# Reordering the first batch's heads, hashes and bursts in a hash-attention and max-out FFN kernel, with four smaller edits

## The chip, the cores and the metric

One NeuronCore of a Trainium2 chip runs the whole program, in one launch. The metric is the device time of one execution, in microseconds. The kernel before takes 272.56 us in the median of three runs (272.11 to 272.76).

## What is computed

Attention over 4 batches, 8 heads, 768 rows and 64 dimensions, in which a query sees only the keys that fall in its own hash bucket, and then a feed-forward network (FFN) that takes the maximum of three products.

```python
q_bits = (np.einsum('bhsd,dk->bhsk', q, proj) > 0)      # 6 bits; the same for k
mask = q_bucket[:, :, :, None] == k_bucket[:, :, None, :]
scores = np.where(mask, scale * q @ k.T, -1e9)
attn = softmax(scores) @ v
x = attn.transpose(0, 2, 1, 3).reshape(B * S, H * D)    # 3072 x 512
out = maximum(maximum(x @ w1, x @ w2), x @ w3) @ w_out   # 512 -> 768 -> 512
```

## The kernel before

**Units.** The work on the scores is cut into 192 units, 48 a batch. A unit is one head, one chunk of queries and a part of the keys. In batch 0 a chunk has 256 queries (three chunks, two units for each head and chunk), in the later batches 384 (two chunks, three units). `scores(u)` (L279) multiplies keys by queries on TensorE into one of two PSUM buffers `sc` (L295), and ScalarE takes the exponential into one of 24 tiles `AT` (L303). The hash bits, as +0.5 and -0.5, stand as 6 or 8 more rows under the 64 dimensions in the S tiles, so that one product gives score and mask together. Each AT tile also has, behind each block of columns, columns of ones, with which a burst sums V. Their place depends on the width of the chunk: a tile that first served 256 wide blocks gets new ones by a memset when it first serves 384 wide ones (L300 to L302, on VectorE, just ahead of the exponential).

**Order of the units** (L258, L259): in batch 0 heads 0 to 3 one after the other, each with its three chunks, then heads 4 to 7 chunk by chunk; later batches go chunk by chunk.

**Getting heads ready.** In batch 0 queries and keys come in pairs of heads 0 to 3: TensorE turns them (`pair_turn`, L122), VectorE or ScalarE copies them (`pair_keep`, L131, L129), GpSimd narrows them into the S tiles (`pair_place`, L136), and a hash makes the bits: `head_rest` for one head (L169 on TensorE, four L174 on VectorE) or `pair_hash` for a pair (L149, L152, then four DMAs by SyncE, L158). Later heads come in quads of four: loads by GpSimd or SyncE (L194), 32 x 32 transposes on VectorE (`turn`, L200), narrowing on GpSimd (L205), placing by DMA on SyncE (L210), and `quad_hash` (L219, L222, four DMAs at L230).

**Bursts.** When four heads of a chunk have their exponentials, a burst makes the row sums (`sums`, L350, then L357 to L361 on VectorE) and the products with V in two sides (`values`, L372, then L379). The second side gives back the AT tiles. In batch 0 the bursts of heads 0 to 3 go in three pieces each, at hand-set units. From batch 1 on VectorE first adds the three parts of a head (`add`, L326, from chunk 5 on also L329), so that `sums` has less to do.

**FFN.** `ffn_groups(c)` (L390) makes 18 groups of four matmuls (L401) for a chunk, each with a copy or maximum after it (L406, L408, L410), then halves of three matmuls with the output weights (L445). A group takes one of four PSUM banks `ms`, as do turns, hashes and bursts.

**The order written out by hand** stands from L460 on. A prologue brings head 0; then for each unit u the loop issues `scores(u + 1)`, what `when(u, ...)` has put down for u, about one FFN group (credit 1, later 1.15 a unit), and the burst pieces due at u. A quad's hash is issued at the end of its unit, its DMAs in the next. Every engine works through its own instructions in that order. After the loop come the last burst, the FFN groups left over, and the FFN of the last chunk. `SPREAD` sets at which units the quads of batches 2 and 3 are transposed.

Of the kernel before, what the change touches and what calls it, by code (L numbers as in the profile page):

```python
# [17 lines left out]
def kernel(  # L18
# [12 lines left out]
    nc = tc.nc  # L31
    B, H, S, D = q.shape
# [3 lines left out]
    HALF = S // 2  # L36
# [14 lines left out]
    SCALE = 0.125 / (RS * RS)  # L51
    EPS = 2.0 ** -60
    NAT = 24
    SPREAD = {2: (61, 9), 3: (100, 12)}
    THIRD_ADD = 5
    LAG = (1, 4)
    ATW = 776
# [36 lines left out]
    def give(i):  # L94
        free_banks.append(i)
# [159 lines left out]
    def parts_of(c):  # L255
        return chunks[c][2] * NM // (2 * HALF)

    order = [(c, h) for h in range(4) for c in range(3)] + [(c, h) for c in range(3) for h in range(4, H)]  # L258
    order += [(c, h) for c in range(3, NCH) for h in range(H)]  # L259
    units = [(c, h, n) for c, h in order for n in range(parts_of(c))]  # L260
    NU = len(units)
# [76 lines left out]
    def burst(c, i):  # L338
# [24 lines left out]
        def values(side, m0, m1):  # L363
# [10 lines left out]
            if m1 == NM:  # L374
                if first:
                    sv_of[b, i, side] = small.tile([P, 1], FP32, tag=f"sv{side}", name="sv")
                    nc.vector.tensor_scalar(out=sv_of[b, i, side][:], in0=av[:, w : w + 1], scalar1=EPS, scalar2=None,
                                            op0=AluOp.mult)
                nc.vector.scalar_tensor_tensor(out=xt_of(c)[:, 2 * i + side, 0:w], in0=av[:, 0:w],  # L379
                                               scalar=sv_of[b, i, side][:], in1=rb[0][:, 0:w], op0=AluOp.add, op1=AluOp.mult)  # L380
                give(held[side][0])
                if side == 1:
                    for h in range(4 * i, 4 * i + 4):
                        for n in range(parts_of(c)):
                            at_free.append(at_of[unit_at[c, h, n]])

        return sums, values

# [71 lines left out]
    with tc.manual_schedule():  # L460
# [41 lines left out]
        head_hash(mk, 0, 1, 0, (1,))  # L502
        head_bits(mk, 0, 1, 0, 1)
        give(ik)
        scores(0)
        pair_turn(0, 1, 1, bk)
        head_hash(mq, 0, 0, 0, (1,))
        head_bits(mq, 0, 0, 0, 1)
        give(iq)
        pair_turn(0, 0, 1, bq)  # L510
        pair_keep(0, 1, 1, bk)
        give(ib)
# [6 lines left out]
        for x in range(4):  # L519
            nc.gpsimd.tensor_copy(pj[x * Q : (x + 1) * Q, :, x : x + 4 * NBITS - 3 : 4], pst[:])  # L520

        for pi, us in ((1, ((0, 1, 0), (0, 0, 0), (3, 1, 1), (4, 0, 1))), (2, ((6, 1, 0), (7, 1, 1), (8, 0, 0), (9, 0, 1))),
                       (3, ((13, 1, 0), (14, 1, 1), (15, 0, 0), (16, 0, 1)))):
            for u, side, hd in us:
                when(u, pair_group, pi, side, hd, nc.scalar if pi == 1 and hd == 1 else None)
                if pi == 1:
                    for par in range(2):
                        when(u, pair_place, pi, side, par, hd, hd + 1)
                elif hd == 1:
                    for par in range(2):  # L530
                        when(u, pair_place, pi, side, par)
        when(2, head_rest, 0, 1)
        when(2, t32.pop, 0)
        when(5, head_rest, 1, 0)
        when(10, pair_hash, 2)
        when(11, t32.pop, 2)
        when(11, head_rest, 1, 1)
        when(12, t32.pop, 1)
        when(17, pair_hash, 3)
        when(18, t32.pop, 3)  # L540
        when(17, load_v, 1)
        for n, u in ((0, 3), (1, 12), (2, 21), (3, 31)):
            when(u, load_weights, n)
# [4 lines left out]
        for g in range(2, NQUAD):  # L548
            b2, i2 = divmod(g, 2)
            need = UPB * b2 + 12 * i2  # L550
            for n, side in enumerate((1, 0)):
# [9 lines left out]
                    if n2 % 2:  # L561
                        when(u2 + 1, narrow, name, n2 // 2)
                when(us[3] + 3, place, name, range(4))
            hash_at[{2: 33, 3: 47}.get(g, need - 9)] = g
            when({2: 36, 3: 46}.get(g, need - 22), load_v, g)

        ffn, credit = [], 0
# [2 lines left out]
        for c, i in sorted(done_at, key=lambda e: done_at[e]):  # L570
# [1 line left out]
            sums, values = burst(c, i)  # L572
            pieces = [lambda f=sums: f(0, NM), lambda f=values: f(0, 0, NM), lambda f=values: f(1, 0, NM)]
            for n, f in enumerate(pieces):
                u = {(0, 0): (20, 21, 22), (1, 0): (24, 25, 26), (2, 0): (28, 29, 30)}.get((c, i), (d, d, d))[n]
                todo.setdefault(u, []).append(f)
            last_of[c] = max(u, last_of.get(c, 0))
        ffn_at = {}
# [5 lines left out]
                when(min(u + 2, NU - 1), add, c, h, n)  # L584

        for u in range(NU):
            if u + 1 < NU:
                scores(u + 1)
            for f in at.pop(u, []):
                f()  # L590
# [10 lines left out]
            if u in hash_at:  # L601
                when(u + 1, quad_hash(hash_at[u]))

        for u in sorted(todo):
            for f in todo[u]:
                f()
# [33 lines left out]
```

## Time and profile before

| what | value |
| --- | --- |
| median of 3 runs | 272.56 us |
| the profiled execution's own time | 272.63 us |
| its span, first to last instruction | 270.9 us |
| TensorE matmuls busy | 259.4 us |
| VectorE busy | 208.9 us |
| ScalarE busy | 177.6 us |
| GpSimd busy | 68.4 us |
| granted TensorE clock | 1.000 |

In the profile, PE is TensorE's matmuls, PEld its weight loads, DVE VectorE, ACT ScalarE, POOL GpSimd and SP SyncE. L295 is line 295 of the kernel before. A row of the timeline gives the start, the time from start to end, engine and line, the operation, output and inputs by the program's names, and how many instructions of the same kind are merged; in brackets stands how long the engine was idle before it, and what ended that. The ends of matmuls are modelled and overlap the next start, so that a price of TensorE work is taken from one start to the next. A row of waits gives who waited for whom, the total in us, how often, and the longest. A row of windows gives the stretch, its length, and then the busy time of PE, PEld, DVE, ACT and POOL, the granted clock, the busy share of the DMA engines and GB/s. A row of DMA issues ends with the median time from issue to landing.

### The profile page before, as it was taken

To read this page: it belongs to the slowest core of one execution; us is meant where nothing else is said; L and a number is where in the kernel's file an instruction comes from. 1 tells how busy PE (TensorE), PEld (TensorE's weight loads), DVE (VectorE), ACT (ScalarE), POOL (GpSimd) and SP (SyncE) were. 2 spreads that over 40 slices of the span, in tenths; PEclk is the share of its full clock that TensorE was granted. 3 is DMA by queue.
4 is the path that set the end of the run, shared out by engine and by line. 5 is a ranking of instruction groups with operands and counts; after the bars stand their busy time and mean duration, and the time that the engine had idled before them with its cause. 6 is when DMAs were issued, how large, how long until landed. Compare 5 with 4: busy or idle time off the path is not lost.

```text
span 270.9 us, 6455 instructions
## 1 busy us (share of the span) xinstructions
PE 259.4 (96%) x2505; PEld 154.5 (57%) x2505; DVE 208.9 (77%) x517; ACT 177.6 (66%) x257; POOL 68.4 (25%) x108
## 2 busy tenths in 40 slices
PE   7899999999989999979999999999999999998995
PEld 3555567865756575545555555565555655554553
DVE  2777686967699899948999998799849795887351
ACT  3587776676939693963959768484895859580322
POOL 3489641272032435140141512011000000000000
PEclk9999999999999999999999999999999999999999
DMA  6969999959623863980036291801130003000303
GB/s 204 315 137 160 221 255 229 229 80 250 150 72 88 156 173 38 235 218 20 11 91 202 30 205 69 169 11 46 29 116 2 2 2 116 2 0 2 116 0 116
DMA packets 20717, 30.95 MB, mean 114 GB/s; under 512 B 2608, under 2 KB 15248, under 8 KB 20688
## 3 DMA queue, kind: packets, MB, share of 16 engines
q0 software_dynamic: 8128, 13.37, 26.3%
q1 hardware_dynamic: 12128, 16.66, 21.1%
q10 hardware_dynamic: 432, 0.52, 0.5%
q8 instruction: 19, 0.31, 0.5%
q14 instruction: 10, 0.08, 0.1%
HBM read 25.17 MB, written 6.29 MB: 116 GB/s over the span
## 4 chain that ended last, share of the span: by engine, by line
PE 86%; DVE 5%; ACT 3%; DMA 2%; POOL 2%; issue 1%; SPq 0%; DVEq 0%; ACTq 0%; POOLq 0%
PE ms L401 32%; PE sc L295 22%; PE ms L372 11%; PE ms L445 10%; PE ms L350 3%; PE ms L219 3%; ACT AT L303 3%; DMA S<-bits 2%; PE ms L483 1%; POOL S L136 1%; PE ms L149 1%; PE ms L122 1%; DVE ad L326 1%; PE ms L169 1%; DVE S L174 1%
## 5 line engine op out<-in xcount | busy, mean ns | idle before, releaser
L303 ACT ACTIVATE AT<-sc 128x768 f16<-128x768 f32 x192 | 152.7, 816 | 65.6 <-PE sc L295 57.9
L401 PE MATMUL ms<-xT,w_sb 128*128 128x384 f16 (+1 forms) x648 | 115.0, 307 | 0.0
L295 PE MATMUL sc<-S 72*128 72x384 bf16 (+1 forms) x432 | 93.5, 308 | 5.4 <-ACT AT L303 2.5
L401 PEld LDWEIGHTS <-w_sb 128*128 128x128 f16 x648 | 62.6, 97 | 35.8 <-issue 0.3
L410 DVE TENSOR_TENSOR ht<-ht,ms 128x384 f16<-128x384 f16 (+1 forms) x108 | 54.2, 504 | 26.0 <-PE ms L401 23.1
L295 PEld LDWEIGHTS <-S 72*128 72x128 bf16 (+1 forms) x432 | 39.4, 98 | 38.0 <-issue 14.1
L205 POOL TENSOR_SCALAR T<-T 128x768 bf16<-128x768 f32 x24 | 22.9, 953 | 105.2 <-DVE T L200 64.5
L372 PE MATMUL ms<-AT,vo 128*32 128x385 f16 (+3 forms) x864 | 35.5, 309 | 0.0
L445 PE MATMUL ms<-wout_sb,ht 128*128 128x512 f16 x138 | 35.3, 378 | 0.0
L372 PEld LDWEIGHTS <-vo 128*32 128x32 f16 x864 | 22.8, 96 | 10.5 <-issue 2.9
L326 DVE TENSOR_TENSOR ad<-ad,AT 128x768 f16<-128x768 f16 x48 | 26.6, 553 | 1.8 <-ACT AT L303 1.1
L200 DVE STREAM_TRANSPOSE T<-nat 128x384 f32<-128x384 f32 x48 | 26.9, 565 | 0.0
L326 DVE TENSOR_TENSOR ad<-AT,AT 128x768 f16<-128x768 f16 x48 | 26.2, 546 | 0.4 <-ACT AT L303 0.4
L406 ACT CAST ht<-ms 128x384 f16<-128x384 f32 x36 | 17.2, 477 | 8.8 <-PE ms L401 8.8
L379 DVE SCALAR_TENSOR_TENSOR xT<-ms,sv,rb 128x384 f16<-128x384 f32 (+1 forms) x36 | 19.8, 567 | 1.6 <-PE ms L372 0.2
L445 PEld LDWEIGHTS <-ht 128*128 128x128 f16 x138 | 13.3, 97 | 13.0 <-DVE ht L410 0.4
L449 ACT COPY osb<-ms 128x512 f32<-128x512 f32 x21 | 12.2, 582 | 8.3 <-PE ms L445 7.2
L329 DVE TENSOR_TENSOR ad<-ad 128x384 f16<-128x384 f16 x32 | 15.5, 484 | 1.1
L136 POOL TENSOR_SCALAR S<-T 64x384 bf16<-64x384 f32 (+1 forms) x23 | 14.2, 617 | 4.7 <-DVE T L131 3.1
L357 DVE STREAM_TRANSPOSE ys<-ms 128x384 f32<-128x384 f32 (+1 forms) x18 | 9.6, 535 | 6.5 <-PE ms L350 6.4
L174 DVE TENSOR_SCALAR S<-ms 6x384 bf16<-6x384 f32 x16 | 8.9, 554 | 3.8 <-PE ms L169 3.5
L194 POOL DMA_DIRECT2D nat<-in_q_dram x20 | 11.1, 564 | 2.1 <-DMA vo<-in_v_dram 2.0
(48 smaller groups left out, 122.8 us busy)
## 6 DMA issues: line engine op xcount, KB each, us to landing
out_dram<-osb SPq DMA_DIRECT2D x21, 256.0 KB
S<-T SPq DMA_DIRECT2D x48, 96.0 KB
nat<-in_q_dram POOLq DMA_DIRECT2D x20, 192.0 KB, 7.3
vo<-in_v_dram POOLq DMA_DIRECT2D x8, 384.0 KB, 6.4
nat<-in_k_dram POOLq DMA_DIRECT2D x16, 192.0 KB, 6.5
w_sb<-in_moe_w_dram POOLq DMA_DIRECT2D x3, 768.0 KB, 7.6
nat<-in_k_dram SPq DMA_DIRECT2D x10, 192.0 KB
nat<-in_k_dram SPq DMA_DIRECT2D x3, 384.0 KB
```

The costliest lines, as they stand in the source:

```text
L136: nc.gpsimd.tensor_scalar(out=o, in0=i_, scalar1=RS, scalar2=1.0, op0=AluOp.mult, op1=AluOp.mult)
L200: nc.vector.transpose(t32[name][:, u, half * HALF : (half + 1) * HALF], i_)
L205: nc.gpsimd.tensor_scalar(out=t16[name][:, u, :], in0=t32[name][:, u, :], scalar1=RS, scalar2=1.0, op0=AluOp.mult, op1=AluOp.mult)
L295: nc.tensor.matmul(views[j], s_of[kn][0 : D + bits, kx, m * P : (m + 1) * P], s_of[qn][0 : D + bits, qx, q0 : q0 + w], start=True, stop=True)
L303: nc.scalar.activation(t[:, :, 0:w], whole, ActFn.Exp, bias=-SCALE * 0.25 * bits, scale=SCALE)
L326: nc.vector.tensor_tensor(out=sum_of[c, h][:], in0=t[0], in1=t[n], op=AluOp.add)
L372: nc.tensor.matmul(av[Q * x : Q * (x + 1), 0:n], v_at[2 * b + i][:, x, cb * D + side : (cb + 1) * D : 2], weights_of(c, 4 * i + x, m)[:, 0 ...
L379: nc.vector.scalar_tensor_tensor(out=xt_of(c)[:, 2 * i + side, 0:w], in0=av[:, 0:w], scalar=sv_of[b, i, side][:], in1=rb[0][:, 0:w], op0=A ...
L401: nc.tensor.matmul(ps[:, 0:w], w_sb[wi][:, jc, fb * P : (fb + 1) * P], xt[:, jc, 0:w], start=(jc == 0), stop=(jc == NJC - 1))
L406: nc.scalar.copy(hts[fb][:, 0:w], ps[:, 0:w])
L410: nc.vector.tensor_tensor(out=hts[fb][:, 0:w], in0=hts[fb][:, 0:w], in1=ps[:, 0:w], op=AluOp.max)
L445: nc.tensor.matmul(ps[:, 0:DM], hts[fb][:, tb * P : (tb + 1) * P], wout_sb[:, fb, :], start=(fb == 0), stop=(fb == NFB - 1))
```

## The change

In batch 0, heads 2 and 3 go chunk by chunk, so that the first chunk's four heads are done at unit 15 in place of 19, and the second's at 19 in place of 21. The first three bursts, in nine pieces, move from units 20 to 30 to units 16 to 29. The turns of pair 2's queries move one unit back and those of pair 3 one or two units forward; the hash of head 3 (`head_rest`, pair 1, second head) moves from unit 11 to 8, that of pair 2 from 10 to 12, that of pair 3 from 17 to 18. In the prologue the second half of head 0's query hash goes ahead of the first scores, and the scores of unit 1 go ahead of head 1's turns.

Four edits stand outside this: the transposes of batch 3 start three units earlier; the columns of ones of the 384 wide blocks are written by GpSimd, right after the burst that gives the tile back, for 24 tiles; the hashes of quads 4 to 7 go 12 units ahead of their first use in place of 9; and after the loop three FFN groups go ahead of the last burst.

```diff
-    SPREAD = {2: (61, 9), 3: (100, 12)}
+    SPREAD = {2: (61, 9), 3: (97, 12)}
...
-    order = [(c, h) for h in range(4) for c in range(3)] + [(c, h) for c in range(3) for h in range(4, H)]
+    order = [(c, h) for h in range(2) for c in range(3)] + [(c, h) for c in range(3) for h in (2, 3)]
+    order += [(c, h) for c in range(3) for h in range(4, H)]
...
                 if side == 1:
                     for h in range(4 * i, 4 * i + 4):
                         for n in range(parts_of(c)):
-                            at_free.append(at_of[unit_at[c, h, n]])
+                            a = at_of[unit_at[c, h, n]]
+                            if b == 0 and i == 1:
+                                nc.gpsimd.memset(blocks(at_tiles[a], HALF)[:, :, HALF : HALF + 2], 1.0)
+                                at_form[a] = HALF
+                            at_free.append(a)
...
         head_bits(mk, 0, 1, 0, 1)
         give(ik)
-        scores(0)
-        pair_turn(0, 1, 1, bk)
         head_hash(mq, 0, 0, 0, (1,))
         head_bits(mq, 0, 0, 0, 1)
         give(iq)
+        scores(0)
+        scores(1)
+        pair_turn(0, 1, 1, bk)
         pair_turn(0, 0, 1, bq)
...
-        for pi, us in ((1, ((0, 1, 0), (0, 0, 0), (3, 1, 1), (4, 0, 1))), (2, ((6, 1, 0), (7, 1, 1), (8, 0, 0), (9, 0, 1))),
-                       (3, ((13, 1, 0), (14, 1, 1), (15, 0, 0), (16, 0, 1)))):
+        for pi, us in ((1, ((0, 1, 0), (0, 0, 0), (3, 1, 1), (4, 0, 1))), (2, ((6, 1, 0), (7, 1, 1), (9, 0, 0), (10, 0, 1))),
+                       (3, ((11, 1, 0), (13, 1, 1), (14, 0, 0), (15, 0, 1)))):
...
-        when(10, pair_hash, 2)
-        when(11, t32.pop, 2)
-        when(11, head_rest, 1, 1)
-        when(12, t32.pop, 1)
-        when(17, pair_hash, 3)
-        when(18, t32.pop, 3)
+        when(8, head_rest, 1, 1)
+        when(9, t32.pop, 1)
+        when(12, pair_hash, 2)
+        when(13, t32.pop, 2)
+        when(18, pair_hash, 3)
+        when(19, t32.pop, 3)
...
-            hash_at[{2: 33, 3: 47}.get(g, need - 9)] = g
+            hash_at[{2: 33, 3: 47}.get(g, need - 12)] = g
...
-                u = {(0, 0): (20, 21, 22), (1, 0): (24, 25, 26), (2, 0): (28, 29, 30)}.get((c, i), (d, d, d))[n]
+                u = {(0, 0): (16, 17, 20), (1, 0): (21, 22, 24), (2, 0): (26, 27, 29)}.get((c, i), (d, d, d))[n]
...
-            if u + 1 < NU:
+            if 0 < u < NU - 1:
                 scores(u + 1)
...
+        for f in ffn[:3]:
+            f()
+        ffn = ffn[3:]
         for u in sorted(todo):
             for f in todo[u]:
                 f()
```

## The prediction

> **What bounds the kernel now.** I read the page first, for the engine that carries the span, then the waits of TensorE, then the places where it stood still.
>
> ```profile
> PE 259.4 (96%) x2505; PEld 154.5 (57%) x2505; DVE 208.9 (77%) x517; ACT 177.6 (66%) x257; POOL 68.4 (25%) x108
> ```
> ```profile
> PE sc L295 <- ACT AT L303: 2.5, 4, 1.2
> PE sc L295 <- DMA S<-bits: 1.7, 1, 1.7
> ```
> TensorE bounds the span at 259.4 of 270.9 us, and the change leaves its matmuls as they are. So it can win only idle time: the waits in its timeline, of which the view of waits puts these two first, and idle time that the modelled ends of matmuls hide. The 2.5 us on ScalarE stand at four places; these two the change touches:
>
> ```profile
> 64.22 0.49 PE L295 MATMUL sc<-S 72*128 72x384 bf16 x2 [0.43 <-ACT AT L303]
> ```
> ```profile
> 81.50 0.48 PE L295 MATMUL sc<-S 72*128 72x384 bf16 x2 [1.22 <-ACT AT L303]
> ```
> The hidden part lies in the first batch. Busy time by stretch, 12.4 to 42.6 us (span, then PE, PEld, DVE, ACT, POOL) and, for later, 73.3 to 113.7:
>
> ```profile
> 12.40:42.60 30.20, 29.32 (x445) 18.59 (x442) 23.15 (x55) 23.77 (x33) 22.21 (x37) 1.00 0.98 199
> 73.30:113.70 40.40, 38.83 (x397) 25.02 (x395) 37.92 (x101) 27.60 (x37) 15.33 (x21) 1.00 0.55 121
> ```
> The first row calls TensorE busy for 29.32 of 30.20 us. Priced from one start to the next, its work is less:
>
> ```profile
> 11.62 0.83 PE L169 MATMUL ms<-T,pj 128*6 128x384 f32 x8
> 12.39 0.50 PE L295 MATMUL sc<-S 70*128 70x256 bf16 x3
> 12.73 0.49 PE L122 MATMUL ms<-iden,nat 128*128 128x128 f32 x3
> 13.06 0.38 PE L295 MATMUL sc<-S 70*128 70x256 bf16 x2
> ```
> ```profile
> 18.49 1.84 PE L149 MATMUL ms<-T,pj 128*32 128x384 f32 x8
> 20.26 0.50 PE L295 MATMUL sc<-S 70*128 70x256 bf16 x3
> ```
> ```profile
> 25.47 1.24 PE L149 MATMUL ms<-T,pj 128*32 128x384 f32 x8
> 26.64 0.39 PE L295 MATMUL sc<-S 70*128 70x256 bf16 x2
> ```
> ```profile
> 32.44 0.84 PE L350 MATMUL ms<-AT,ones 128*32 128x256 f16 x24
> 33.21 0.50 PE L295 MATMUL sc<-S 70*128 70x256 bf16 x3
> 33.64 0.40 PE L372 MATMUL ms<-AT,vo 128*32 128x256 f16 x8
> ```
> ```profile
> 40.33 0.84 PE L350 MATMUL ms<-AT,ones 128*32 128x256 f16 x24
> ```
> ```profile
> 42.56 0.50 PE L295 MATMUL sc<-S 70*128 70x256 bf16 x3
> ```
> A head_rest takes 12.39 - 11.62 = 0.77 us, a unit's scores 0.34, a turn 0.33, a pair_hash 26.64 - 25.47 = 1.17, a burst piece 0.77 and 33.64 - 33.21 - 0.34 = 0.09 for the switch, the whole burst at unit 32 2.23. From the scores of unit 4 (12.39) to those of unit 34 (42.56) that is 30 x 0.34 + 10 x 0.33 + 2 x 0.77 + 2 x 1.17 + 9 x 0.86 + 2.23 = 27.4 us, and it took 30.17. So about 2.8 us of hidden idle time lie there. One piece shows: the first pair_hash took 20.26 - 18.49 = 1.77 us, 0.6 more than the second, since its last input was copied late (below).
>
> **The change part by part.**
>
> *Start.* Where the scores of units 0 and 1 stand now, and the bits that they need:
>
> ```profile
> 7.94 0.49 PE L295 MATMUL sc<-S 70*128 70x256 bf16 x3 [1.06 <-DVE S L174]
> ```
> ```profile
> 9.81 0.38 PE L295 MATMUL sc<-S 70*128 70x256 bf16 x2
> ```
> ```profile
> 6.66 1.73 DVE L174 TENSOR_SCALAR S<-ms 6x384 bf16<-6x384 f32 x3 [0.90 <-PE ms L169]
> ```
> The third bits of that row end at 8.39, so the scores of unit 1 could start at 8.45 in place of 9.81. The moved query hash fits into the 1.06 us wait. Then both units' scores and head 1's two turns are through at 8.45 + 3 x 0.33 = 9.44, in place of 9.81 + 0.34 = 10.15; of these 0.7 us I take 0.6. ScalarE then paces the units:
>
> ```profile
> 21.99 1.51 ACT L303 ACTIVATE AT<-sc 128x768 f16<-128x768 f32 x2 [0.39 <-PE sc L295]
> ```
> Two exps in 1.51 us, overlapped by a tenth, are about 0.7 a unit, so the 0.6 us is handed on as long as nothing else stops TensorE.
>
> *Hashes dealt anew.* VectorE works in order through what the hashes need:
>
> ```profile
> 15.20 2.26 DVE L174 TENSOR_SCALAR S<-ms 6x384 bf16<-6x384 f32 x4 [0.37 <-PE ms L169]
> 17.49 1.95 DVE L131 COPY T<-ms 128x384 f32<-128x384 f32 x4
> ```
> Four bits take 2.26 us and a copy 0.49. Now head_rest(1, 0) is followed by four copies and pair_hash(2). Afterwards head_rest(1, 1) comes at unit 8, between the key and the query copies of pair 2. With 0.6 us won, VectorE starts at 14.6 and ends the last query copy at 14.6 + 2.26 + 2 x 0.49 + 2.26 + 2 x 0.49 = 21.1. So pair_hash(2), at unit 12, waits longer than now, and ends near 21.5. The 0.6 us is lost there. But by then the scores of unit 13 are issued, not 11, and head_rest(1, 1) is behind: those of unit 14 start near 21.6. From there to unit 34 lie 20 x 0.34 + 3 x 0.33 + 1.17 + 9 x 0.86 + 2.23 = 18.9 us of TensorE work, and I leave some 0.6 us for waits on ScalarE, whose 0.7 a unit is more than the 0.34 + 0.33 of units 14 to 17. The burst pieces now stand from unit 16 on, where TensorE would wait for ScalarE. Unit 34 comes at 41.1, against 42.56: **1.45 us**. Between no gain and all of the hidden time, 2.8, I take it because the one late copy is in it.
>
> Two deadlines come nearer. Hash 3 moves back to unit 18, and its bits must land by unit 28:
>
> ```profile
> 27.34 0.72 SPq L158 DMA_DIRECT2D S<-bits  x1
> ```
> ```profile
> SPq L194 <- DMA S<-bits: 2.0, 1, 2.0
> ```
> ```profile
> 34.37 0.79 SPq L194 DMA_DIRECT2D nat<-in_q_dram  x2
> ```
> ```profile
> 35.62 0.50 PE L295 MATMUL sc<-S 70*128 70x256 bf16 x3
> ```
> SyncE waited for a bits transfer until 34.37, so the one issued at 27.34 took up to 7.0 us; the scores of unit 28 came at 35.62. Afterwards hash 3 ends near 21.6 + 6 x 0.34 + 3 x 0.33 + 2 x 0.86 + 1.17 + 0.1 = 27.6, is issued 0.7 later as now (27.34 - 26.64), at 28.3, and lands by 35.3. The scores of unit 28 are ready at 41.1 - 6 x 0.34 - 2 x 0.86 - 2.23 = 35.1: up to 0.2 us of wait. The bits of quad 2 have a like deadline at unit 48. I take 0.2 us off for both: **1.25 us**. The Trainium skill, DMA: Bandwidth & Descriptors, section Anatomy of one DMA, gives a transfer (issued by GpSimd) about 2 us of fixed cost beside its bytes; by that the bits would land at 30.3, nothing would come off, and the sum would be 4.85 (an estimate). The 7.0 us here, with the DMA engines 0.98 busy in that stretch, does not agree.
>
> *Columns of ones by GpSimd.* Now VectorE writes them just before the exp:
>
> ```profile
> ACT AT L303 <- DVE AT L301: 5.4, 4, 3.3
> ```
> ScalarE waited 5.4 us, behind VectorE's queue, and through the two score buffers this made the 0.43 and 1.22 us of TensorE above. Afterwards GpSimd writes them as soon as the burst has read the tile, far ahead of the exp: the burst of unit 32 ends at 42.56, and its tiles serve units 48 to 55. GpSimd has the time (22.21 of 30.20 and 15.33 of 40.40 busy). Behind its waiting memsets stand a narrow, the loads of V and of batch 2's heads, whose cover is the work of the units in between: no cost. Were it gone, VectorE would wait ahead of L200. VectorE is next: it had 40.40 - 37.92 = 2.5 us free where TensorE is to go 1.2 us faster, and already sets one wait (L326) of 0.35:
>
> ```profile
> 104.09 0.35 PE L350 MATMUL ms<-ad,ones 128*32 128x384 f16 x4 [0.35 <-DVE ad L326]
> ```
> I give back 0.5 us: 0.43 + 1.22 - 0.5 = **1.15 us**, between 0.43 and 2.0.
>
> *Quad hashes three units earlier.* The chain that ended last goes through this transfer to unit 96:
>
> ```profile
> 110.56 6.55 DMA S<-bits
> ```
> Three units, none shorter than ScalarE's 0.7 us, bring it 2.1 us or more forward, and the burst of unit 87 no longer stands ahead of it. So the 1.7 us wait goes. Batch 3's transposes three units earlier (SPREAD) keep ahead of their hashes; VectorE has the same number of them. **1.5 us**, 0.2 kept for VectorE's backlog, which the wait had let drain; 1.0 to 1.7.
>
> *Tail.* Three FFN groups go ahead of the last burst:
>
> ```profile
> 243.69 0.34 PE L350 MATMUL ms<-ad,ones 128*32 128x384 f16 x3
> 245.19 0.32 PE L350 MATMUL ms<-ad,ones 128*32 128x384 f16 x1 [1.16 <-DVE ad L329]
> ```
> ```profile
> 247.39 0.82 PE L401 MATMUL ms<-xT,w_sb 128*128 128x384 f16 x4
> 248.05 4.05 PE L445 MATMUL ms<-wout_sb,ht 128*128 128x512 f16 x18
> 251.94 0.49 PE L401 MATMUL ms<-xT,w_sb 128*128 128x384 f16 x2
> ```
> ```profile
> 245.05 0.55 DVE L410 TENSOR_TENSOR ht<-ht,ms 128x384 f16<-128x384 f16 x1
> ```
> They are one L401 group (248.05 - 247.39 = 0.66) and two halves of L445 (3.89 / 6 = 0.65 each). From 243.6 the L401 group ends at 244.3, the first half at 244.9, two thirds of the second at 245.3. Its last third needs the maximum that VectorE makes after the one at 245.05, so at 246.1. The burst then starts at 246.3, ends at 248.5, and four halves end at 251.1, against 251.94. **0.75 us**, between 0.3 and the full 1.2 (1.16). VectorE then has 2.6 us, the four halves, to make the last xT, where it had 4.55 (251.94 - 247.39).
>
> Sum: 1.25 + 1.15 + 1.5 + 0.75 = 4.65 us. The profiled execution took 272.63 us (span 270.9), 0.07 above the median of 272.56. That gives 267.9.
>
> **The rivals.**
>
> *VectorE takes over* in units 60 to 96. For it: 37.92 of 40.40 busy, and the wait at 104.09. Against it: 2.5 us free, 24 fewer memsets. Then the ones are worth 0.43 and the earlier hash 1.0: 1.25 + 0.43 + 1.0 + 0.75 = 3.4, or 269.2 us. Chance 0.17.
>
> *The new order does nothing in the first batch*: the late copy holds pair_hash(2) for longer, or the bits eat the rest. Against it: 2.8 us of hidden idle. 1.15 + 1.5 + 0.75 = 3.4, again 269.2 us. Chance 0.13.
>
> *All idle time comes back*: 2.1 in the first batch (1.45 and the 0.6 of the start), 1.65, 1.7 and 1.2, together 6.6, or 266.0 us. Chance 0.12.
>
> *Slower: hash 3's bits land too late for unit 28.* They are issued at 28.3 behind four loads of the query quad that GpSimd now issues after a pair_place, 1.5 us later than now, and beside V and the third weights:
>
> ```profile
> w_sb<-in_moe_w_dram POOLq DMA_DIRECT2D x3, 768.0 KB, 7.6
> ```
> If they land only after two transfers of that kind in turn, 15.2 us, that is at 43.5 and 8.4 us late: 4.65 less 8.4 is 3.75 slower, 276.3 us. It decides from 39.75, that is 35.1 plus 4.65. The 7.0 us of now speak against it. Chance 0.06.
>
> **How the numbers follow.** The forecast, 267.9, has 0.50, with 266.9 to 269.0 as its own range. The rivals have 0.17, 0.13, 0.12 and 0.06; 0.02 is left for several small losses together. The range 265.9 to 270.6 takes in the first three, and the first two at once (1.25 less: 270.4); about 0.15 lies outside. A measurement of this kernel tells some 0.2% from no change. Faster by more: 0.92; within it 0.02; slower 0.06.
>
> **What would show each step.** Start: unit 1's scores near 8.45. Order: unit 34's near 41.1, a pair_hash L149 of about 2 us near 19.5 to 21.5, no wait of L295 for S<-bits near 35. Ones: no ACT wait for L301, the gaps at 64 and 81 gone, waits for ad L326 below 1 us in all. Hash: no gap at unit 96. Tail: the gap before the last burst moved and about 0.8 us. The prediction is wrong if a wait for S<-bits or for VectorE in units 60 to 96 takes more than 1 us, or if unit 34 comes after 42 us.

## The result and the profile after

The changed kernel takes 269.15 us in the median (268.93 to 269.28), beside 272.66 us for the kernel before on the same chip: a ratio of 0.9864, 95% interval 0.9831 to 0.9898. That is 3.5 us faster, where 4.65 were forecast. The profiled execution took 269.28 us (span 267.3). The matmuls are the same 2505; what went is idle time of TensorE. The page's line of busy time, after:

```profile
PE 259.6 (97%) x2505; PEld 153.7 (58%) x2505; DVE 208.8 (78%) x493; ACT 177.9 (67%) x257; POOL 70.0 (26%) x132
```

VectorE has lost its 24 memsets (517 to 493 instructions), GpSimd has got them (108 to 132). The lines of the kernel shift: L295 is now L296, L303 L304, L326 L327, L350 L351, L372 L373, L401 L406, L410 L415 and L445 L450. TensorE's waits, after (total, times, longest):

```profile
PE ms L450 <- DVE ht L415: 1.6, 3, 0.8
PE ms L488 <- DVE pj L477: 1.1, 1, 1.1
PE sc L296 <- DVE S L174: 0.6, 2, 0.4
PE ms L149 <- DVE S L174: 0.4, 1, 0.4
PE sc L296 <- ACT AT L304: 0.3, 1, 0.3
```

Of the two waits that led the list before, 2.5 us of scores on ScalarE and 1.7 us on S<-bits, 0.3 us are left. A new one leads, FFN matmuls that wait for VectorE's maximum (L415).

The start of unit 0 itself moves from run to run: 7.94 us in the trace of before, 8.26 in that of after, 7.64 to 8.64 over all the traces, while the units after it repeat to 0.02 us in programs that are the same up to there, wherever no transfer is waited for. So I count from there. When the scores of a unit start, in us after those of unit 0, and what each stretch has won:

| unit | before | after | won so far | won in the stretch |
| --- | --- | --- | --- | --- |
| 4 | 4.45 | 3.84 | 0.61 | 0.61 |
| 34 | 34.62 | 33.90 | 0.72 | 0.11 |
| 48 | 48.90 | 48.19 | 0.71 | -0.01 |
| 52 | 56.28 | 54.98 | 1.30 | 0.59 |
| 72 | 78.11 | 75.27 | 2.84 | 1.54 |
| 74 | 80.06 | 77.98 | 2.08 | -0.76 |
| 85 | 92.30 | 90.21 | 2.09 | 0.01 |
| 96 | 109.21 | 105.14 | 4.07 | 1.98 |
| 103 | 120.50 | 116.66 | 3.84 | -0.23 |
| 139 | 167.29 | 163.69 | 3.60 | -0.24 |
| 151 | 183.96 | 180.60 | 3.36 | -0.24 |
| last chunk's FFN | 244.00 | 240.16 | 3.84 | 0.48 |
| end | 262.91 | 259.05 | 3.86 | 0.02 |

So the first batch gave 0.71 us, the ones 1.38 (units 48 to 85), the stretch with the hash 1.98, the tail 0.48, and three steps of 0.24 took back 0.71. With the last 0.02 that is 3.86 us; unit 0 was 0.32 later in this execution, which leaves 3.5.

**First batch.** TensorE from the start, after, and the scores of unit 34:

```profile
8.26 0.49 PE L296 MATMUL sc<-S 70*128 70x256 bf16 x3 [0.40 <-DVE S L174]
8.95 0.49 PE L296 MATMUL sc<-S 70*128 70x256 bf16 x3 [0.20 <-DVE S L174]
...
42.16 0.50 PE L296 MATMUL sc<-S 70*128 70x256 bf16 x3
```

Unit 1 is now 0.69 us behind unit 0. TensorE at pair_hash(2), after:

```profile
20.56 1.89 PE L149 MATMUL ms<-T,pj 128*32 128x384 f32 x8 [0.37 <-DVE S L174]
22.38 0.50 PE L296 MATMUL sc<-S 70*128 70x256 bf16 x3
```

And VectorE in the same stretch:

```profile
14.90 2.26 DVE L174 TENSOR_SCALAR S<-ms 6x384 bf16<-6x384 f32 x4 [0.36 <-PE ms L169]
17.20 1.02 DVE L131 COPY T<-ms 128x384 f32<-128x384 f32 x2
18.25 2.26 DVE L174 TENSOR_SCALAR S<-ms 6x384 bf16<-6x384 f32 x4
20.54 1.49 DVE L131 COPY T<-ms 128x384 f32<-128x384 f32 x3
```

Bits, two copies, bits, copies, in the order that the prediction gave. The hash first waits 0.37 us for the second bits to free a bank, starts when they end (18.25 + 2.26 = 20.51), and stands through the copies behind them: 1.82 us from its start to the next scores, where the prediction's rows have 1.17 for one that nothing holds.

**VectorE behind the ones.** The gaps of 0.43 and 1.22 us on ScalarE are gone. TensorE between the scores of units 73 and 74, after, has a gap that was not there before:

```profile
84.84 0.60 PE L450 MATMUL ms<-wout_sb,ht 128*128 128x512 f16 x2
86.02 0.39 PE L450 MATMUL ms<-wout_sb,ht 128*128 128x512 f16 x1 [0.58 <-DVE ht L415]
```

The third matmul of this half needs a maximum that VectorE started at 85.55, behind an addition of batch 1 and a transpose:

```profile
84.62 0.57 DVE L200 STREAM_TRANSPOSE T<-nat 128x384 f32<-128x384 f32 x1
85.11 0.51 DVE L327 TENSOR_TENSOR ad<-ad,AT 128x768 f16<-128x768 f16 x1
85.55 0.41 DVE L415 TENSOR_TENSOR ht<-ht,ms 128x256 f16<-128x256 f16 x1
```

**The steps of 0.24 us** lie after units 96, 132 and 144, where the hash of quads 5 to 7 now stands alone. Before, it stood right behind a burst:

```profile
169.74 0.35 PE L350 MATMUL ms<-ad,ones 128*32 128x384 f16 x4
...
171.87 1.46 PE L219 MATMUL ms<-T,pj 128*32 128x384 f32 x16
173.26 0.50 PE L295 MATMUL sc<-S 72*128 72x384 bf16 x2
```

After, the same hash and the same burst apart:

```profile
160.93 0.81 PE L450 MATMUL ms<-wout_sb,ht 128*128 128x512 f16 x3
161.57 0.49 PE L296 MATMUL sc<-S 72*128 72x384 bf16 x2
161.90 0.81 PE L450 MATMUL ms<-wout_sb,ht 128*128 128x512 f16 x3
162.64 1.50 PE L219 MATMUL ms<-T,pj 128*32 128x384 f32 x16
164.07 0.50 PE L296 MATMUL sc<-S 72*128 72x384 bf16 x2
...
167.75 0.35 PE L351 MATMUL ms<-ad,ones 128*32 128x384 f16 x4
...
169.98 0.50 PE L296 MATMUL sc<-S 72*128 72x384 bf16 x2
```

The figure behind the names is the part of TensorE's array that a matmul uses, rows by columns: hash and burst use 32 columns at a time (`128*32`), scores and FFN all 128 (`72*128`, `128*128`). Three FFN matmuls take 161.57 - 160.93 = 0.64 us up to scores, but 162.64 - 161.90 = 0.74 up to a hash: 0.1 us for the change. Burst and hash together took 173.26 - 169.74 = 3.52 us; apart they take 1.43 + 2.23 = 3.66, 0.14 more. Together 0.24. The Trainium skill, TensorEngine Tiling (Array Packing), section Key Properties, says that changing the tiling mode, and not just the tile, drains TensorE. These rows agree with that, and put about 0.1 us on one change.

**Tail.** TensorE from the three groups to the last chunk's FFN, after:

```profile
241.21 1.24 PE L450 MATMUL ms<-wout_sb,ht 128*128 128x512 f16 x5
243.27 0.39 PE L450 MATMUL ms<-wout_sb,ht 128*128 128x512 f16 x1 [0.83 <-DVE ht L415]
243.59 0.35 PE L351 MATMUL ms<-ad,ones 128*32 128x384 f16 x4
...
245.82 2.76 PE L450 MATMUL ms<-wout_sb,ht 128*128 128x512 f16 x12
248.42 3.90 PE L406 MATMUL ms<-xT,w_sb 128*128 128x384 f16 x23
```

The burst no longer waits for its additions, but the last third of the second half waits 0.83 us for a maximum, and the burst starts 4.66 us after unit 191, where before it started 1.72 us after it.

### The profile page after: what moved, and what is told of

Read it like the earlier page. It is cut to its first block, busy times and chain, and to the rows that moved or that the text cites. A ratio compares the mean times of both kernels' runs of the same rounds, so it can differ in the third digit from the quotient of the medians.

```text
span 267.3 us, 6477 instructions
## 1 busy us (share of the span) xinstructions
PE 259.6 (97%) x2505; PEld 153.7 (58%) x2505; DVE 208.8 (78%) x493; ACT 177.9 (67%) x257; POOL 70.0 (26%) x132
## 4 chain that ended last, share of the span: by engine, by line
PE 84%; DVE 9%; ACT 3%; issue 2%; DVEq 0%; ACTq 0%
PE ms L406 31%; PE sc L296 21%; PE ms L373 11%; PE ms L450 10%; PE ms L219 3%; PE ms L351 3%; ACT AT L304 3%; DVE ht L415 2%; DVE ad L327 2%; PE ms L122 1%; PE ms L488 1%; PE ms L149 1%; DVE S L174 1%; DVE T L131 1%; DVE xT L380 1%
## 5 line engine op out<-in xcount | busy, mean ns | idle before, releaser
L304 ACT ACTIVATE AT<-sc 128x768 f16<-128x768 f32 x192 | 152.5, 815 | 61.0 <-PE sc L296 57.0
L406 PE MATMUL ms<-xT,w_sb 128*128 128x384 f16 (+1 forms) x648 | 114.8, 307 | 0.1
L296 PE MATMUL sc<-S 72*128 72x384 bf16 (+1 forms) x432 | 93.8, 309 | 1.3 <-DVE S L174 0.6
L406 PEld LDWEIGHTS <-w_sb 128*128 128x128 f16 x648 | 62.7, 97 | 35.9 <-issue 0.4
L415 DVE TENSOR_TENSOR ht<-ht,ms 128x384 f16<-128x384 f16 (+1 forms) x108 | 54.2, 503 | 21.6 <-PE ms L406 18.6
L296 PEld LDWEIGHTS <-S 72*128 72x128 bf16 (+1 forms) x432 | 39.2, 98 | 33.7 <-issue 14.8
L205 POOL TENSOR_SCALAR T<-T 128x768 bf16<-128x768 f32 x24 | 22.9, 953 | 91.0 <-issue 47.8
L450 PE MATMUL ms<-wout_sb,ht 128*128 128x512 f16 x138 | 36.0, 379 | 1.6 <-DVE ht L415 1.6
L373 PE MATMUL ms<-AT,vo 128*32 128x385 f16 (+3 forms) x864 | 35.2, 309 | 0.0
L327 DVE TENSOR_TENSOR ad<-ad,AT 128x768 f16<-128x768 f16 x48 | 26.5, 552 | 1.8 <-ACT AT L304 1.1
L373 PEld LDWEIGHTS <-vo 128*32 128x32 f16 x864 | 22.4, 96 | 9.2 <-issue 1.3
L327 DVE TENSOR_TENSOR ad<-AT,AT 128x768 f16<-128x768 f16 x48 | 26.2, 546 | 0.4 <-ACT AT L304 0.4
L450 PEld LDWEIGHTS <-ht 128*128 128x128 f16 x138 | 13.3, 97 | 15.7 <-DVE ht L415 3.0
```

Source lines behind the costliest of these rows:

```text
L205: nc.gpsimd.tensor_scalar(out=t16[name][:, u, :], in0=t32[name][:, u, :], scalar1=RS, scalar2=1.0, op0=AluOp.mult, op1=AluOp.mult)
L296: nc.tensor.matmul(views[j], s_of[kn][0 : D + bits, kx, m * P : (m + 1) * P], s_of[qn][0 : D + bits, qx, q0 : q0 + w], start=True, stop=True)
L304: nc.scalar.activation(t[:, :, 0:w], whole, ActFn.Exp, bias=-SCALE * 0.25 * bits, scale=SCALE)
L327: nc.vector.tensor_tensor(out=sum_of[c, h][:], in0=t[0], in1=t[n], op=AluOp.add)
L373: nc.tensor.matmul(av[Q * x : Q * (x + 1), 0:n], v_at[2 * b + i][:, x, cb * D + side : (cb + 1) * D : 2], weights_of(c, 4 * i + x, m)[:, 0 ...
L406: nc.tensor.matmul(ps[:, 0:w], w_sb[wi][:, jc, fb * P : (fb + 1) * P], xt[:, jc, 0:w], start=(jc == 0), stop=(jc == NJC - 1))
```

## The experiments

My theory on the result was the prediction's own: four separate pieces of idle time, each taken back by its own edit. The rivals: the first batch gives nothing, all of it comes from the four smaller edits; VectorE has taken over; and, for the wait ahead of unit 96, that something else than the earlier hash removed it. All ratios are against the kernel before on the same chip, with the 95% interval. Where a run is compared with the changed kernel, the two medians come from different chips, on which the kernel before had medians of 272.5 to 272.9 us. A difference of a few tenths of a microsecond between such medians decides nothing by itself; what carries the comparison is the time between units in the traces.

**1 and 2. Each half alone.** *mends_only* is the kernel before with the four edits outside the first batch; *first_batch_only* is the changed kernel without them. The four edits:

```diff
-    SPREAD = {2: (61, 9), 3: (100, 12)}
+    SPREAD = {2: (61, 9), 3: (97, 12)}
...
+                            if b == 0 and i == 1:
+                                nc.gpsimd.memset(blocks(at_tiles[a], HALF)[:, :, HALF : HALF + 2], 1.0)
+                                at_form[a] = HALF
...
-            hash_at[{2: 33, 3: 47}.get(g, need - 9)] = g
+            hash_at[{2: 33, 3: 47}.get(g, need - 12)] = g
...
+        for f in ffn[:3]:
+            f()
+        ffn = ffn[3:]
```

> The kernel before with the four smaller edits alone (first batch as before). Theory T, from the two traces' ledger: the first batch's new order is worth 0.4 us at unit 34, the four edits 3.1, so 269.5 us. Rival P, the prediction's split: the first batch is worth 1.25 and the four edits only what is left of the measured 3.5, 2.3, so 270.4 us. Under T the scores of units 4 to 48 come within 0.1 us of the kernel before, unit 103 some 3.1 us earlier than there. A third reading, that the first scores' 0.3 us later start in the changed kernel is only a scatter of the first loads, expects unit 0 anywhere from 7.9 to 8.3 here too.

> The changed kernel without the four smaller edits: the first batch's new order alone. Theory T: unit 34 at about 42.2 and the whole 0.4 us faster than before, 272.2 us, if the DMA wait ahead of unit 96 keeps it. Rival P: unit 34 at 41.1 to 41.5 and 271.3 us. A rival N says that what is won early is eaten by the later waits on VectorE and on the hash transfer: 272.6 us, no difference.

Measured: mends_only 269.96 us, 0.9894 (0.9865 to 0.9924); first_batch_only 271.79, 0.9962 (0.9935 to 0.999). The halves add up, 2.7 and 0.9 us against 3.5 for both. The first batch does give something, if little. In first_batch_only the wait of before ahead of unit 96 stands, 1.3 us, and the scores of unit 28 waited 0.53 us, which those of the changed kernel did not:

```profile
35.76 0.49 PE L296 MATMUL sc<-S 70*128 70x256 bf16 x3 [0.53 <-POOL T L205]
```

Nothing in that half can have caused this, since both programs are the same up to there. The row names GpSimd's narrowing (L205), but the scores of unit 28 don't need it: in the changed kernel they start while that narrowing still runs.

```profile
35.42 0.50 PE L296 MATMUL sc<-S 70*128 70x256 bf16 x3
```
```profile
35.06 0.83 POOL L205 TENSOR_SCALAR T<-T 128x768 bf16<-128x768 f32 x1 [0.40 <-DVE T L200]
```

They need the bits of hash 3. By the landings recorded in the traces, the pieces of the second of its four transfers landed at 34.06 to 34.21 us in first_batch_only, except for one, at 35.62, which is 0.14 us ahead of the scores. In the changed kernel all of them had landed by 34.52. The mends_only trace has such a wait too, although its first batch is that of the kernel before: unit 28 came 28.18 us after unit 0, against 27.68, and unit 34 35.35, against 34.62, so its expectation of equal times up to unit 48 missed. The late piece is thus not the new order's doing.

**3. pair_hash(2) one unit later** (*hash2_at_13*), so that VectorE is through with the copies when the hash comes.

```diff
-        when(12, pair_hash, 2)
-        when(13, t32.pop, 2)
+        when(13, pair_hash, 2)
+        when(14, t32.pop, 2)
```

> The changed kernel with pair_hash(2) one unit later, at unit 13. Theory V: it stood 1.2 us at unit 12 because VectorE, behind the four bits of head_rest(1, 1), had not made the copies and freed the PSUM bank; with one unit more of scores and a turn between, it takes about 1.4 us in place of 1.9, and unit 34 comes 0.5 to 0.9 us earlier, at 41.3 to 41.7; whole 268.4 us. Rival S: the stretch up to unit 34 is bound by ScalarE's 0.7 a unit and TensorE's own work, and the wait only moves: unit 34 within 0.2 of 42.16, whole 269.1 us.

Measured: 269.01 us, 0.9852 (0.9817 to 0.9887). TensorE in it:

```profile
20.65 1.21 PE L149 MATMUL ms<-T,pj 128*32 128x384 f32 x8
21.80 0.50 PE L296 MATMUL sc<-S 70*128 70x256 bf16 x3
...
34.43 0.49 PE L296 MATMUL sc<-S 70*128 70x256 bf16 x3 [0.23 <-DMA S<-bits]
```

The hash takes 1.15 us now, without a wait, and unit 24 comes 0.67 us earlier than in the changed kernel (23.14 after unit 0, against 23.81). So VectorE's copies did hold it. But 0.3 us of this is gone by unit 34 (33.52 against 33.90), with a wait of 0.23 for the bits of hash 3 at unit 28, and the time stays the same within its interval.

**4. Hash 3 one unit earlier too** (*hash3_at_17*), to bring its bits forward.

```diff
-        when(18, pair_hash, 3)
-        when(19, t32.pop, 3)
+        when(17, pair_hash, 3)
+        when(18, t32.pop, 3)
```

> The changed kernel with pair_hash(2) at unit 13 and pair_hash(3) at unit 17 in place of 18, so that its bits are sent one unit, about 1.2 us, earlier. Theory B: the wait ahead of unit 28 (0.23 us with pair_hash(2) alone moved, 0.4 to 0.5 in two other kernels) is the bits' landing by their issue; it goes, and unit 34 comes 33.2 to 33.3 us after unit 0, against 33.52 with pair_hash(2) alone moved and 33.90 in the changed kernel. Rival Q: the bits land with the query quad's loads that GpSimd issued ahead of them, whenever they are sent: the wait stays within 0.1 us, unit 34 at 33.5 after unit 0.

Measured: 269.01 us, 0.9869 (0.9854 to 0.9883). The wait for the bits went, and another came: unit 17 now holds the hash and a burst piece, the units behind it come with little between them, and TensorE reaches the scores of unit 21 before ScalarE has freed their buffer.

```profile
28.18 0.49 PE L296 MATMUL sc<-S 70*128 70x256 bf16 x3 [0.57 <-ACT AT L304]
```

**5. The burst piece out of unit 17** (*first_batch_mended*), with 3 and 4 kept.

```diff
-                u = {(0, 0): (16, 17, 20), (1, 0): (21, 22, 24), (2, 0): (26, 27, 29)}.get((c, i), (d, d, d))[n]
+                u = {(0, 0): (16, 18, 20), (1, 0): (21, 22, 24), (2, 0): (26, 27, 29)}.get((c, i), (d, d, d))[n]
```

> The changed kernel with pair_hash(2) at unit 13, pair_hash(3) at unit 17 and the second piece of the first burst at unit 18 in place of 17. Theory: the 0.5 us that pair_hash(3) at unit 17 lost (a wait of 0.57 us on ScalarE) came from a hash and a burst piece in one unit, and the wait ahead of unit 28 from hash 3's bits; with both apart, unit 24 comes 23.1 to 23.2 us after unit 0 and unit 34 33.2 to 33.3 us, 0.6 us ahead of the changed kernel's 33.90, whole 268.5 us. Rival: ScalarE's or VectorE's pace binds there anyway and unit 34 stays at 33.5 to 33.7.

Measured: 268.5 us, 0.9822 (0.9784 to 0.9859). Both waits are gone, and unit 34 comes at 33.23 after unit 0, 0.67 before that of the changed kernel and 1.39 before that of the kernel before. So the 0.67 us that pair_hash(2) cost can be had, if nothing behind it becomes late. In run 12 the same edits met late bits.

**6. The ones back on VectorE** (*ones_on_vector*).

```diff
-                            if b == 0 and i == 1:
-                                nc.gpsimd.memset(blocks(at_tiles[a], HALF)[:, :, HALF : HALF + 2], 1.0)
-                                at_form[a] = HALF
```

> The changed kernel with the columns of ones written by VectorE just before the exp, as before; all else as changed. Theory of the ledger: the two gaps of 0.43 and 1.22 us near units 52 and 67 come back, and the waits near 86 and 109.6 shrink, since VectorE gets ahead again: 0.6 to 1.3 us more, 269.8 to 270.4 us. Rival V2: VectorE bounds units 60 to 96 in either place and the move is worth nothing: 269.1 us.

Measured: 270.5 us, 0.9923 (0.9903 to 0.9942), 1.35 us more than the changed kernel. The old gap is back in the trace, and the gap of 0.58 us at unit 74 is not there:

```profile
81.45 0.48 PE L296 MATMUL sc<-S 72*128 72x384 bf16 x2 [1.22 <-ACT AT L304]
```

From unit 48 to 72 this kernel is 2.13 us behind the changed one, from unit 74 on 1.37. So the edit wins 2.13 us and VectorE's backlog takes 0.76 of it.

**7. Less work for VectorE** (*casts_on_scalar*): the first copies of the FFN groups of chunks 1 and 2 go to ScalarE, 12 copies of 0.41 us.

```diff
-                    if w == HALF:
+                    if w == HALF or c:
                         nc.scalar.copy(hts[fb][:, 0:w], ps[:, 0:w])
```

> The changed kernel with the twelve first copies of the FFN's chunks 1 and 2 on ScalarE in place of VectorE (0.42 us each, 5 us of VectorE's work in units 56 to 95 gone). Theory V: the two waits of L450 for L415 near 86 and 109.6 us, after which 0.8 and 0.3 us of lead are lost, are VectorE's backlog; they go, unit 96 comes about 1.1 us earlier, 268.0 us. Rival: it is the chain of those very maxima behind TensorE, not the backlog, or ScalarE's exps now come later: within 0.3 us of 269.1.

Measured: 268.17 us, 0.9837 (0.9822 to 0.9852), 1.0 us less than the changed kernel. No gap of TensorE is left in its trace between 60 and 112 us. Unit 74 comes 0.73 us earlier (77.25 after unit 0) and unit 96 1.0 (104.14). So the backlog was VectorE's, and it cost 1.0 us in all: 0.7 at unit 74 and 0.3 at unit 93.

**8. The hashes back behind bursts, that of quad 4 kept early** (*hashes_with_bursts*). The transposes go back to unit 100 with it; these two go together.

```diff
-    SPREAD = {2: (61, 9), 3: (97, 12)}
+    SPREAD = {2: (61, 9), 3: (100, 12)}
...
-            hash_at[{2: 33, 3: 47}.get(g, need - 12)] = g
+            hash_at[{2: 33, 3: 47, 4: 84}.get(g, need - 9)] = g
```

> The changed kernel with the hashes of quads 5 to 7 back at 9 units ahead, right behind a burst, and the transposes of batch 3 at 100 as before, since these two go together; quad 4's hash stays early at unit 84. Theory H: a hash by itself costs TensorE 0.24 us more than one right behind a burst, three times, since the change between full-width and 32-wide matmuls costs about 0.1 us each time: 0.7 us less, 268.4 us, with the steps of 0.23, 0.24, 0.24 after units 96, 132 and 144 gone. Rival D: the steps are VectorE's backlog, and they stay wherever the hash stands: 269.1 us.

Measured: 268.53 us, 0.9843 (0.9808 to 0.9877), 0.62 us less than the changed kernel. Against it units 103, 139 and 151 come 0.23, 0.47 and 0.71 us earlier: exactly the three steps. The run moves the transposes as well, and the hash of quad 4 shows which of the two it is. Behind the burst, in the kernel before and in hash4_at_87 (run 9, transposes from 100 and from 97), the products with V and the hash take 3.35 and 3.36 us up to the scores. Apart, in this run and in the changed kernel (from 100 and from 97), they take 2.06 + 1.43 = 3.49 and 2.05 + 1.43 = 3.48, and the FFN group ahead of the hash takes 0.53 us in place of 0.44. So the price goes with the hash's place.

**9 and 10. Which edit removed the wait ahead of unit 96?** In *hash4_at_87* the hash of quad 4 alone is late again, with batch 3's transposes still early. In *both_hash_edits_undone* both are as before, and the ones and the first batch stay changed.

```diff
-            hash_at[{2: 33, 3: 47}.get(g, need - 12)] = g
+            hash_at[{2: 33, 3: 47, 4: 87}.get(g, need - 12)] = g
```

```diff
-    SPREAD = {2: (61, 9), 3: (97, 12)}
+    SPREAD = {2: (61, 9), 3: (100, 12)}
...
-            hash_at[{2: 33, 3: 47}.get(g, need - 12)] = g
+            hash_at[{2: 33, 3: 47}.get(g, need - 9)] = g
```

> The changed kernel with quad 4's hash back at unit 87, behind the burst, all else as changed. Theory C: the wait of the scores of unit 96 for S<-bits comes back, 1.7 us or more since these scores now come earlier, and 0.24 us are won where the hash stands behind the burst again: from unit 85 to 96 16.4 to 16.9 us in place of 14.9, whole 270.6 to 271.1 us. Rival: VectorE's backlog takes most of what the earlier hash gave, so that undoing it costs under 1 us: 269.2 to 270.0 us.

> The changed kernel with batch 3's transposes back at unit 100 and the hashes of quads 4 to 7 back at 9 units ahead; everything else of the change is kept. The changed kernel takes 269.15 us and has no wait for S<-bits ahead of unit 96. With the hash alone put back to unit 87 (269.45 us) there was none either, and with the hash at 84 and the transposes at unit 100 (268.53 us) none. Theory (the wait needs both: the late hash, and the loads of batch 3's heads by GpSimd issued in the same microseconds as the bits): now both hold, as in the kernel before, and the wait of the kernel before (1.69 us) comes back, 1.3 to 1.7 us; from the scores of unit 85 to those of unit 96 it takes 16.3 to 17 us in place of 14.93. The hashes of quads 5 to 7 stand next to bursts again, which gives back 3 x 0.24 = 0.7 us. Time 269.8 to 270.4 us. Rival (the wait had gone because VectorE has the ones no longer, or the first batch is ordered anew, and neither hash edit mattered): no wait of L296 for S<-bits, 15.0 us from unit 85 to unit 96, and 268.4 to 268.7 us.

Measured: hash4_at_87 269.45 us, 0.9859 (0.9816 to 0.9902), both_hash_edits_undone 270.03, 0.9877 (0.9822 to 0.9933). From unit 85 to unit 96 it took:

| hash of quad 4 at unit | batch 3's transposes from | 85 to 96, us | wait for S<-bits, us |
| --- | --- | --- | --- |
| 87 (before) | 100 | 16.91 | 1.7 |
| 87 (both_hash_edits_undone) | 100 | 16.64 | 1.4 |
| 87 (hash4_at_87) | 97 | 15.07 | none |
| 84 (hashes_with_bursts) | 100 | 14.93 | none |
| 84 (after) | 97 | 14.93 | none |

Either edit removes the wait; only with neither does it stand. The expectation of hash4_at_87 missed: the hash alone, put back, brought no wait. TensorE and the chain of the end in both_hash_edits_undone, then a narrowing and loads on GpSimd:

```profile
112.69 1.47 PE L406 MATMUL ms<-xT,w_sb 128*128 128x384 f16 x8
115.56 0.50 PE L296 MATMUL sc<-S 72*128 72x384 bf16 x2 [1.41 <-DMA S<-bits]
```
```profile
109.24 6.27 DMA S<-bits
```
```profile
102.38 1.05 POOL L205 TENSOR_SCALAR T<-T 128x768 bf16<-128x768 f32 x1 [3.12 <-DVE T L200]
...
104.28 2.19 POOL L194 DMA_DIRECT2D nat<-in_k_dram  x4
```

And its DMA engines from 110 to 115 us (the last three columns: clock, busy share of the DMA engines, GB/s):

```profile
110.00:115.00 5.00, 4.15 (x23) 2.03 (x21) 4.33 (x8) 4.29 (x7) 2.40 (x3) 1.00 0.93 230
```

In hash4_at_87 SyncE issues the same bits at the same time, but three of the four loads went 5 us earlier. SPREAD sets the units of the loads as well as those of the transposes (14 units ahead of them), and three units earlier they stand ahead of the narrowing, not behind it:

```profile
99.37 1.67 POOL L194 DMA_DIRECT2D nat<-in_k_dram  x3
102.44 1.04 POOL L205 TENSOR_SCALAR T<-T 128x768 bf16<-128x768 f32 x1 [1.40 <-DVE T L200]
...
104.33 0.56 POOL L194 DMA_DIRECT2D nat<-in_k_dram  x1
```
```profile
107.77 2.92 SPq L230 DMA_DIRECT2D S<-bits  x4
```
```profile
110.00:115.00 5.00, 5.00 (x29) 2.71 (x28) 4.38 (x9) 4.75 (x8) 2.35 (x3) 1.00 0.36 126
```
```profile
114.05 0.49 PE L296 MATMUL sc<-S 72*128 72x384 bf16 x2
```

By the landings recorded in the two traces, the last bits land at 112.66 us here, and at 115.72 in both_hash_edits_undone (the transfer that unit 96 waited for at 115.51), with the DMA engines 0.36 and 0.93 busy. So the wait is not the lateness of the hash alone: it is bits and loads in flight together. The Trainium skill, DMA: Bandwidth & Descriptors, section Queues, rings and completion order, says that a DMA engine takes turns between the queues that have work for it, a packet at a time; the loads of GpSimd and the bits of SyncE are in two queues, and the pair of runs agrees with that. The rule does not give the 3 us.

**11. Two FFN groups ahead of the last burst in place of three** (*tail_two_groups*).

```diff
-        for f in ffn[:3]:
+        for f in ffn[:2]:
             f()
-        ffn = ffn[3:]
+        ffn = ffn[2:]
```

> The changed kernel with two FFN groups ahead of the last burst in place of three. Theory G: the third group is the second half of an L450 product and waits 0.83 us for the maximum that VectorE makes behind the last adds, as the prediction's tail had it; with two groups the burst starts when its sum is ready, near 242.1 in the changed kernel's time, and the last chunk's FFN begins 0.5 to 0.8 us earlier: 268.5 us. Rival W: the wait only moves to the burst's last sum or to the last xT, so the last chunk's FFN begins within 0.2 us: 269.1 us.

Measured: 269.12 us, 0.9868 (0.9851 to 0.9886), the same as the changed kernel. In its trace the wait of 0.83 us is gone, and from unit 191 to the last chunk's FFN it takes 9.00 us in place of 9.49:

```profile
241.68 0.81 PE L450 MATMUL ms<-wout_sb,ht 128*128 128x512 f16 x3
242.42 0.53 PE L351 MATMUL ms<-ad,ones 128*32 128x384 f16 x4
243.09 2.13 PE L373 MATMUL ms<-AT,vo 128*32 128x384 f16 x48
```

The sums took 0.5 us longer to pass: the last of them needed an addition that ended at 242.57, and the products with V began when a maximum of VectorE (L415) ended at 243.04. That is less than the third group cost. But the profiled execution, 269.28 us and the longest of four, lost 0.6 us by unit 28, as first_batch_only did; whether the others did isn't known, so on the time this run is inconclusive.

**12. All together** (*all_together*): the edits of 3, 4, 5, 7, 8 and 11 on the changed kernel.

> The changed kernel with the first batch mended as in the run of that name, the hashes of quads 5 to 7 behind the bursts and batch 3's transposes at 100, two FFN groups ahead of the last burst, and the copies of chunks 1 and 2 on ScalarE. If the terms add up, 0.65 + 0.71 + 0.49 + 1.0 = 2.85 us less than the changed kernel: 266.3 us. If the engines' slack is shared, VectorE's relief and the earlier units compete and the sum is 1.5 to 2 us: 267.2 to 267.7 us.

Measured: 266.28 us (265.89 to 267.54), 0.9747 (0.9709 to 0.9785), which beats both kernels: the one before by 6.6 us on the same chip, the changed one by 2.9 between medians of two chips. The profiled execution took 267.54 us, the longest of the six, and has the wait at unit 28, longer than in any other run, and one at unit 26:

```profile
33.26 0.81 PE L296 MATMUL sc<-S 70*128 70x256 bf16 x6 [0.58 <-ACT AT L304]
...
35.89 0.49 PE L296 MATMUL sc<-S 70*128 70x256 bf16 x3 [1.04 <-DMA S<-bits]
```

Unit 34 stands at 34.67 after unit 0, 1.44 behind first_batch_mended, whose program is the same up to there. The row puts the first wait down to ScalarE, which ended an exponential at 33.19, but the buffer of unit 26 had been free since 32.49, when the one before that ended; the last bits for unit 26 landed at 33.12 us and those for unit 28 at 35.75, each 0.14 us ahead of its scores. So the landing of these bits differs from one execution to the next by more than 1 us. The start of unit 0 doesn't go with it: it is 8.15 us in tail_two_groups and both_hash_edits_undone, which have the wait, and in casts_on_scalar and first_batch_mended, which have not. What holds the late piece back stays open.

## Why the prediction was right or wrong

**The sum** was 4.65 us and 3.5 came; the time lies in the range and just outside the forecast's own, 266.9 to 269.0. It is also the 269.2 of two rivals, by other terms than theirs. That the total came this near is in part luck: the first batch gave 0.54 us less than forecast, the tail 0.27 less and a missing term took 0.71, while the ones gave 0.23 more and the hash 0.48 more.

**Start: right.** Unit 1's scores came 0.69 us behind unit 0, where before they had been 1.87 behind, and by unit 4 the gain was 0.61 us, where 0.6 was taken. Unit 1's own place was given as 0.51 behind unit 0 (8.45 against 7.94), so it came 0.18 later than that.

**Hashes dealt anew: the step that failed.** The prediction put unit 34 at 41.1 with unit 0 at 7.94, that is 33.16 after it; it came at 33.90. The order of VectorE's work was as forecast, and so was its time to 0.15 us (the hash's last copy, two copies after the bits, ends near 20.54 + 1.02 = 21.56, or 21.24 with unit 0's 0.32 taken off, against 21.1). What stood behind the last copy was too small: the prediction let unit 14's scores start 0.5 us after it, and it took 22.38 - 21.56 = 0.8, since the hash of the last head, whose matmuls start at 21.61 and 21.96, stands whole behind that copy. That, with the small slip ahead of it, made unit 14 0.46 us late; 0.28 more came up to unit 34 (19.78 us in place of 18.9 + 0.6). Runs 3 and 5 showed that the hash could stand a unit later for 0.67 us. What the first batch lacked against the forecast, 1.25 - 0.71 = 0.54, is less than that. That 2.8 us of hidden idle time lay there was not refuted, but half of it, 1.39, is the most that a run took back by unit 34. Of the signs that were set for being wrong, unit 34 after 42 us, the row as it stands meets this one (42.16); without the 0.32 us of unit 0 it is 41.84.

**Deadlines: right in size, wrong in kind.** 0.2 us were taken off for the bits of hash 3 at unit 28. In the changed kernel's profile they cost nothing, in three kernels with the same program up to there (first_batch_only, tail_two_groups, both_hash_edits_undone) 0.5 to 0.6, and in run 12 1.0; mends_only, with the old order, has the wait too. It is a cost that comes in some executions and not in others, with the old order as with the new. The rival that they come 8 us late has nothing for it.

**Columns of ones: right, with both its parts too small.** 1.65 - 0.5 = 1.15 was forecast and 1.37 came, as 2.13 - 0.76 (run 6; the table's stretch has 1.38). The loss was where the prediction had put it, on VectorE in units 60 to 96, and run 7 showed whose it was. The mark that was set for being wrong, more than 1 us of waits for VectorE there, was not passed by the rows (0.58 and 0.16), and just reached by what run 7 got back (1.0).

**VectorE takes over: partly true.** TensorE did wait for it, but the ones kept 1.37 and not 0.43, the hash 1.98 and not 1.0.

**Quad hashes earlier: the gain right, its cause half.** 1.5 us was forecast, 1.98 came. Unit by unit, the scores of unit 96 came 1.85 us sooner behind those of unit 95 without the wait for the bits, and from unit 85 to 92 it took 10.03 us in place of 10.50, since the wait of 0.35 us on an addition went too; the wait for VectorE's maximum ahead of unit 93 took back 0.33. The prediction gave the gain to the hash and nothing to SPREAD, which moves batch 3's transposes and loads. Runs 9 and 10 showed that either does it, and that what was late was the landing beside batch 3's loads.

**A term that was missing.** The prediction moved four hashes and priced only that of quad 4. Those of quads 5 to 7 left the bursts they had stood behind, for 0.24 us each: 0.71 us, shown by run 8. The rows that give it, a hash behind a burst and the scores after it, were in the trace of before.

**Tail: right in mechanism, too large.** 0.75 was forecast, 0.48 came; the term that was too small is the burst's move. The wait of the last third was foreseen as 0.8 us and measured as 0.83; the burst and the four halves took 2.23 and 2.60 us, as forecast (2.2 and 2.6). The three groups moved the burst by 2.94 us (1.72 to 4.66 after unit 191) in place of 2.7.

## What to carry to other kernels

A hash or a small product that uses the array in another tile is cheapest beside others of that tile: who moves it away from them pays for more changes, here 0.24 us a hash. When a transfer lands late, look at what else is in flight at that time before moving its issue, since the loads that it meets can be moved as well. A wait that a row puts down to an engine which had long been done, or whose work the waiting one doesn't need, is another's: look at the landings. Work taken from one engine's queue (the ones) shows the next wait in that same queue; take some more from it (run 7) before calling the gain done.

## What the runs showed of the hardware

The same four bits transfers, issued at the same time (107.7 us), landed 3 us apart with the DMA engines 0.36 or 0.93 busy. A change of TensorE between 128 columns and 32 cost about 0.1 us (0.64 against 0.74 us for the same three matmuls), without any wait in the rows. One piece of a small transfer could land 1.4 us behind its other pieces (35.62 against 34.21 us in first_batch_only), and this differed between executions of the same instructions. The first unit started anywhere from 7.64 to 8.64 us with the same or nearly the same code ahead of it, a scatter as large as several of the terms weighed here.
